# Keeping far-off work out of the opening stretch of a recorded schedule, and a longer guess for DMA transposes

## The chip, the cores and the metric

The kernel runs on one core of one Trainium2 chip, in one launch. The metric is the device time of that launch in microseconds (us), the median of several runs. Before the change it is 729.1 us (three runs, 729.02 to 730.64). Engines are named as in the profile: PE is TensorE (PEld its weight loads), DVE is VectorE, ACT is ScalarE, POOL is GpSimd, SP issues the DMAs.

## The reference

A pre-LayerNorm transformer block on 2048 tokens of width 1024: linear attention with 32 heads of 32, then a gated feed-forward part (F = 3584) with ReLU on the gate. Cut to what is computed:

```python
h  = x + A(_layernorm(x))          # A: qkv = x @ wqkv; phi(q), phi(k) = where(t > 0, t+1, exp(t)) + 1e-6
                                   #    kv = phi(k)^T v, z = sum phi(k); o = phi(q) kv / (phi(q) z + 1e-6); o @ wo
h2 = h + B(_layernorm(h))          # B: relu(x @ W_gate) * (x @ W_up) @ W_down
```

The inputs are bf16, and so is the output.

## The kernel before

The products are done as Strassen-Winograd blocks: seven products of half-size blocks in place of eight, for which DVE makes sums and differences of the blocks of the left operand (the normalized x, "left sums") and of the right operand (the weights). Each group of products ends in PSUM banks that ACT and DVE empty; until a bank has been emptied, PE can't start the next group in it.

All engine calls are recorded first, and then a planner inside the kernel gives them an order. It runs while the program is built, not on the chip: it has a guessed duration for each call, keeps a clock for each engine and one for the DMA wire, and always takes the call that can start first; among those that could start on an engine it takes the one with the smallest `late`, the latest start that by its guess holds nobody up. The order that comes out is fixed, and the engines follow it.

```python
class Plan:
    SEM = 100.0
    WINDOW = 6000.0
    AHEAD = 120000.0
    ...
    def schedule(self):
        nodes = self.nodes
        succs = self.order()            # sets v.late for each recorded call
        ...
        for i, v in enumerate(nodes):
            v.left, v.ready = len(v.preds), max(0.0, v.late - self.AHEAD) if v.dma else 0.0
            if not v.left:
                avail[v.eng].append(i)
        ...
            s, e, a = best
            now = [i for i in a if nodes[i].ready <= s]
            i = min(now, key=lambda i: (nodes[i].nom if e == "tensor" else nodes[i].late, i))
            ...
            v.start = s
            clock[e] = s + v.hold
            end = s + v.hold + v.lat
            if v.dma:
                wire = max(wire, s + v.hold) + v.dma
                end = wire + v.lat - v.dma + min(4000.0, max(0.0, 0.25 * (v.late - s)))
            ...                         # successors become ready at end
```

In the plan times are ns. A DMA transpose from SBUF to SBUF counts as a call of SP with `hold` 1250 and `lat` 2350 and no wire time (`v.dma` is 0).

These are the calls that matter for the opening. Tokens are handled in pairs of 128-token tiles (p and p + 8). Pair 0 is done with plain products, without the seven-product scheme, while the weights are still arriving:

```python
def left_sums(lo, n):                   # for tokens lo .. lo+n of both halves
    c = slice(lo, lo + n)
    a11, a12, a21, a22 = (XH[i][k][:, :, c] for i in range(2) for k in range(2))
    s1, s2, s4, s3 = (a[:, :, c] for a in (*XS, XS3))     # s3 lies over a21
    ...
    return [tt(s1, a21, a22, ALU.add), tt(s2, s1, a11, ALU.subtract),
            tt(s4, a12, s2, ALU.subtract), tt(s3, a11, a21, ALU.subtract)]     # four DVE calls

def k_phi(i, j, ps):                    # phi of a plain product of pair 0
    e = at(156 + 2 * i + j, [512])
    nc.scalar.activation(out=e, in_=ps, func=ACT.Exp)
    def post():
        phi_clamp(e)                                               # DVE, bf16 in place
        phi_join(pk0[:, i, j * 512:(j + 1) * 512], ps, e)          # DVE, reads the bank
    tick.do(lambda: post)

class Norm:                             # LayerNorm of one tile
    def finish(self, on_dve=False):
        self.rstd_()
        xn = self.xn
        (nc.vector if on_dve else nc.gpsimd).tensor_scalar(out=xn, in0=self.x, scalar1=self.negm[:], scalar2=self.rstd[:],
                                op0=ALU.add, op1=ALU.mult)
        nc.sync.dma_start_transpose(out=XI[self.i][:, :, self.r:self.r + P], in_=xn)
        ...

class Quad:                             # one group of seven products
    def p2(self):
        self.prod(self.D, 2, False)
        self.out["c22"](self.E, self.u3)     # DVE add of a bank and a copy; frees the bank
        self.out["c11"](self.D)
    ...

for p in range(1, NP):                  # NP = 8
    ...
    ls = left_sums((p + 1) % NP * P, P)      # at p = 7 these are the sums of pair 0
    ...
```

The left sums of pair 0 are recorded last in this loop (p = 7), since pair 0 needs them only for the products with the weights of q, which come after all of k and v.

Of the kernel before, what the change touches and what calls it, by code (L numbers as in the profile page):

```python
# [32 lines left out]
class Plan:  # L33
# [5 lines left out]
    SEM = 100.0  # L39
    WINDOW = 6000.0  # L40
    AHEAD = 120000.0

    class Node:
        __slots__ = ("eng", "calls", "preds", "hold", "lat", "open", "dma", "late", "ready", "left", "start", "nom")
# [155 lines left out]
    def schedule(self):  # L200
        nodes = self.nodes
        succs = self.order()
        engines = ("tensor", "vector", "scalar", "gpsimd", "sync")
        avail = {e: [] for e in engines}
        clock = {e: 0.0 for e in engines}
        for i, v in enumerate(nodes):
            v.left, v.ready = len(v.preds), max(0.0, v.late - self.AHEAD) if v.dma else 0.0
            if not v.left:
                avail[v.eng].append(i)
        pe = [i for i, v in enumerate(nodes) if v.eng == "tensor"]  # L210
        done, first, wire, out = set(), 0, 0.0, []
        while True:
            best = None
            for e in engines:
                a = avail[e]
                if not a:
                    continue
                if e == "sync":
                    for i in a:
                        v = nodes[i]  # L220
                        if v.late - max(clock[e], v.ready) > 6000.0:
                            v.ready = max(v.ready, wire - 2000.0)
                if e == "tensor":
                    while first < len(pe) and pe[first] in done:
                        first += 1
                    limit = nodes[pe[first]].nom + self.WINDOW
                    a = [i for i in a if nodes[i].nom <= limit]
                    if not a:
                        continue
                s = max(clock[e], min(nodes[i].ready for i in a))  # L230
                if best is None or s < best[0]:
                    best = (s, e, a)
            if best is None:
                break
# [3 lines that stand above are left out]
            v = nodes[i]  # L238
            if e != "tensor":

                soon = [j for j in a if s < nodes[j].ready < s + 0.5 * v.hold and nodes[j].late < v.late - 1500.0]
                if soon:
                    i = min(soon, key=lambda j: (nodes[j].late, j))
                    v = nodes[i]
                    s = v.ready
# [3 lines that stand above are left out]
            if v.dma:  # L249
                wire = max(wire, s + v.hold) + v.dma  # L250
                end = wire + v.lat - v.dma + min(4000.0, max(0.0, 0.25 * (v.late - s)))
            avail[e].remove(i)
            done.add(i)
            out.append(i)
            for j in succs[i]:
                w = nodes[j]
                r = clock[e] if w.eng == e else end
                w.ready = max(w.ready, r)
                w.left -= 1
                if not w.left:  # L260
                    avail[w.eng].append(j)
        assert len(out) == len(nodes)
        self.span = max(clock.values())
        return out
# [1303 lines left out]
```

## Time and profile before

The profiled execution spans 726.4 us. Its page and the windows of its trace say:

| stretch | PE busy | DVE busy | POOL busy | DMA share |
|---|---|---|---|---|
| whole span, 726.4 us | 714.9 us | 564.0 us | 78.2 us | q1: 54.4% of 16 engines |
| 0 to 10 us | 8.14 us | 4.77 us | 1.70 us | 0.78 |
| 10 to 20 us | 9.89 us | 9.68 us | 1.48 us | 1.14 |
| 20 to 28 us | 8.00 us | 6.83 us | 2.99 us | 0.38 |
| 28 to 32 us | 1.16 us | 4.00 us | 2.77 us | 0.44 |
| 32 to 60 us | 27.94 us | 21.85 us | 11.15 us | 0.66 |

A row is read across: in a stretch of 4 us (28 to 32) PE worked 1.16 us, and DVE all of it. A DMA share near or over 1 is read as full queues (the packets' times are added up). Nearly every call goes through one line of the recorder (L121), so lines of code don't tell groups apart, and the operation, the shape and the time of an instruction must.

### The profile page before, as it was taken

How to read it: one execution, taken by the hardware profiler on the slowest of the kernel's cores; microseconds unless marked ns; L12 is line 12 of the kernel's file. 1: busy time of each engine (PE TensorE's matmuls, PEld its weight loads, DVE VectorE, ACT ScalarE, POOL GpSimd, SP SyncE). 2: the span in 40 equal slices, each digit the busy share in tenths (PEclk: the TensorE clock that was granted, in tenths of full speed). 3: DMA queues.
4: the chain of work that ended last, by engine and by line, in shares of the span. 5: the costliest groups of instructions: out<-in, count | busy, mean ns of one | idle time of the engine just before them, and what ended most of it. 6: DMA issues, size and time to landing. Idle time of an engine off the chain costs nothing.

```text
span 726.4 us, 11220 instructions
## 1 busy us (share of the span) xinstructions
PE 714.9 (98%) x4163; PEld 396.9 (55%) x4163; DVE 564.0 (78%) x954; ACT 277.3 (38%) x540; POOL 78.2 (11%) x88
## 2 busy tenths in 40 slices
PE   8899999999999999999999999999999999999998
PEld 3344545444444444444444444444444688888887
DVE  6887745896897785566767968769858879899996
ACT  5788544666555443333333333333333220001100
POOL 1433000002202120000000000000000004101452
PEclk9999999999999999999999999999999999999999
DMA  9555505239776730446146585685681878777974
GB/s 286 157 120 115 148 1 180 54 84 222 160 158 151 142 85 1 122 140 188 51 143 190 154 254 159 197 261 178 206 262 50 268 262 221 205 271 233 247 79 60
DMA packets 156503, 117.40 MB, mean 162 GB/s; under 512 B 54944, under 2 KB 140192, under 8 KB 156320
## 3 DMA queue, kind: packets, MB, share of 16 engines
q1 hardware_dynamic: 148832, 113.01, 54.4%
q0 software_dynamic: 7616, 3.67, 4.9%
q8 instruction: 32, 0.52, 0.3%
q14 instruction: 23, 0.19, 0.1%
HBM read 70.52 MB, written 34.08 MB: 144 GB/s over the span
## 4 chain that ended last, share of the span: by engine, by line
PE 89%; DVE 5%; ACT 3%; DMA 2%; issue 1%; POOL 0%; DVEq 0%; ACTq 0%
PE psum L121 89%; DVE mem L121 4%; ACT mem L121 2%; DMA mem<-mem 2%; DVE tiny L121 1%; ACT tiny L121 0%; POOL mem L121 0%; DVE mem L549 0%; POOL tiny L121 0%; DVEq L121 0%; ACTq L121 0%
## 5 line engine op out<-in xcount | busy, mean ns | idle before, releaser
L121 PE MATMUL psum<-mem 128*128 128x512 f16 (+4 forms) x4147 | 714.0, 335 | 7.9 <-DVE mem L121 3.4
L121 PEld LDWEIGHTS <-mem 128*128 128x128 f16 (+1 forms) x4163 | 396.9, 98 | 325.6 <-issue 10.4
L121 DVE TENSOR_TENSOR mem<-psum,mem 128x512 f32<-128x512 f32 (+2 forms) x240 | 187.1, 792 | 100.8 <-ACT mem L121 67.0
L121 DVE TENSOR_TENSOR mem<-mem 128x512 f16<-128x512 bf16 (+8 forms) x400 | 241.6, 642 | 14.5 <-DMA mem<-mem 9.2
L121 ACT COPY mem<-psum 128x512 f32<-128x512 f32 (+2 forms) x124 | 92.7, 749 | 210.1 <-PE psum L121 202.4
L121 ACT COPY psum<-psum 128x512 f32<-128x512 f32 (+1 forms) x68 | 49.1, 722 | 160.6 <-PE psum L121 147.9
L121 POOL DMA_DIRECT2D out_dram<-mem x28 | 34.1, 1299 | 413.8 <-DVE mem L121 413.7
L121 ACT ACTIVATE mem<-psum 128x512 bf16<-128x512 f32 x90 | 53.6, 598 | 18.2 <-PE psum L121 17.7
L121 POOL TENSOR_SCALAR mem<-mem,tiny 128x1024 bf16<-128x1024 bf16 x28 | 38.2, 1364 | 197.0 <-ACT tiny L121 176.3
L121 DVE SCALAR_TENSOR_TENSOR mem<-mem 128x512 bf16<-128x512 bf16 (+1 forms) x71 | 57.6, 812 | 1.3
L121 DVE SCALAR_TENSOR_TENSOR mem<-psum,mem 128x512 bf16<-128x512 f32 x66 | 45.4, 687 | 11.9 <-PE psum L121 7.9
L121 ACT ACTIVATE mem<-mem,tiny 128x1024 bf16<-128x1024 bf16 x24 | 27.4, 1143 | 11.0 <-DVE tiny L121 5.8
L121 DVE TENSOR_SCALAR mem<-mem 128x512 bf16<-128x512 bf16 (+1 forms) x49 | 16.2, 331 | 18.2 <-ACT mem L121 18.0
L121 DVE TENSOR_TENSOR mem<-psum,tiny 128x384 bf16<-128x384 f32 (+1 forms) x48 | 22.9, 507 | 5.3 <-ACT tiny L121 3.9
L121 ACT ACTIVATE mem<-mem 128x1024 bf16<-128x1024 f32 (+1 forms) x23 | 24.3, 1056 | 6.3 <-DVE mem L121 6.2
L121 ACT ACTIVATE tiny<-tiny 128x1 f32<-128x1 f32 (+2 forms) x112 | 22.8, 206 | 9.2 <-DVE tiny L121 6.3
L121 ACT ACTIVATE tiny<-psum 128x12 f32<-128x12 f32 (+1 forms) x48 | 8.1, 169 | 13.9 <-PE psum L121 13.4
L121 DVE BATCH_NORM_STATS2 tiny<-mem 128x6 f32<-128x512 bf16 x16 | 10.2, 680 | 3.0 <-DMA mem<-in_A_x_dram 3.0
L121 ACT CAST mem<-psum 128x512 bf16<-128x512 f32 x18 | 10.4, 583 | 4.2 <-PE psum L121 3.7
L121 POOL TENSOR_SCALAR tiny<-tiny 128x1 f32<-128x1 f32 x14 | 4.4, 314 | 26.7 <-ACT mem L121 13.5
L121 ACT ACTIVATION_READ_ACCUMULATOR mem<-mem,tiny 128x1 f32 x24 | 4.5, 188 | 0.0
L121 DVE TENSOR_SCALAR tiny<-tiny 128x1 f32<-128x1 f32 x16 | 3.3, 209 | 0.3
(18 smaller groups left out, 14.4 us busy)
## 6 DMA issues: line engine op xcount, KB each, us to landing
l_dram<-mem SPq DMA_DIRECT2D x98, 128.0 KB, 2.3
mem<-l_dram SPq DMA_DIRECT2D x12, 896.0 KB, 6.1
mem<-in_A_x_dram SPq DMA_DIRECT2D x32, 256.0 KB, 3.0
mem<-in_B_W_up_dram SPq DMA_DIRECT2D x14, 512.0 KB, 5.4
mem<-in_B_W_gate_dram SPq DMA_DIRECT2D x14, 512.0 KB, 4.3
mem<-in_B_W_down_dram SPq DMA_DIRECT2D x28, 256.0 KB, 3.8
r_dram<-mem SPq DMA_DIRECT2D x56, 128.0 KB, 1.8
mem<-r_dram SPq DMA_DIRECT2D x8, 896.0 KB, 5.1
```

What stands on the lines that cost most here:

```text
L121: call = lambda: getattr(getattr(self.nc, eng), op)(*args, **k)
```

## The change

The change has two edits, both to the planner; no call is added, removed or altered.

1. A call that isn't PE's and whose `late` lies past 90 us isn't offered before 45 us of planned time. It is meant to keep work that is due much later, such as the left sums of pair 0, from being slipped into gaps of the opening, where the guesses are least sure.
2. A call of SP without wire time, which is a DMA transpose, is expected to end no sooner than 0.8 us after the planned wire is free, but at most 2.5 us later than guessed so far. It is meant to let the plan know that a transpose behind a full wire takes longer.

```diff
@@ class Plan
     AHEAD = 120000.0
+    OPENING = 45000.0
@@ def schedule
             v.left, v.ready = len(v.preds), max(0.0, v.late - self.AHEAD) if v.dma else 0.0
+            if v.eng != "tensor" and v.late > 2.0 * self.OPENING:
+
+                v.ready = max(v.ready, self.OPENING)
             if not v.left:
@@ def schedule
                 end = wire + v.lat - v.dma + min(4000.0, max(0.0, 0.25 * (v.late - s)))
+            elif e == "sync":
+
+                end = max(end, min(wire + 800.0, end + 2500.0))
             avail[e].remove(i)
```

What the two edits do to the order can be read from the two built programs. The orders on PE, ACT, POOL and SP are the same, instruction by instruction. On DVE six of 924 instructions stand elsewhere (times are those of the trace before, to find them by):

| instructions | shape | stood before | stand after | moved by |
|---|---|---|---|---|
| left sums s1, s2 of pair 0 | tensor_tensor, 128x512 | 13.49 and 14.01 us | behind the bank add of 51.03 us | edit 1 |
| left sums s3, s4 of pair 0 | tensor_tensor, 128x512 | 28.20 and 29.38 us | behind those two | edit 1 |
| clamp and join of k's block (0, 1) | tensor_scalar and scalar_tensor_tensor, 128x512 | 23.52 and 23.85 us | ahead of the sums of 21.25 us | edit 2 |

## The prediction

> **What bounds the kernel now.** I read the page first: the busy times, then the chain that ended last.
>
> ```profile
> PE 714.9 (98%) x4163; PEld 396.9 (55%) x4163; DVE 564.0 (78%) x954; ACT 277.3 (38%) x540; POOL 78.2 (11%) x88
> PE 89%; DVE 5%; ACT 3%; DMA 2%; issue 1%; POOL 0%; DVEq 0%; ACTq 0%
> ```
>
> PE is the bound: 714.9 of 726.4 us busy, and the change leaves every matmul and PE's order as it is. So only PE's idle time can move, 11.5 us or 1.6% of the span. A change of 2% is out of reach downwards. The second view is who PE waits for, between 10 and 60 us (total, times, longest):
>
> ```profile
> PE psum L121 <- DVE mem L121: 2.8, 1, 2.8
> ```
>
> It is one wait, and PE's timeline between 28.0 and 32.5 us places it (start, duration, operation, count, idle time before it):
>
> ```profile
> 31.83 1.02 PE L121 MATMUL psum<-mem 128*128 128x512 bf16 x4 [2.84 <-DVE mem L121]
> ```
>
> PE stops at 28.99 and goes on at 31.83, when DVE has emptied a bank. The third view is DVE's timeline before that:
>
> ```profile
> 21.25 2.35 DVE L121 TENSOR_TENSOR mem<-mem 128x512 f16<-128x512 bf16 x4 [1.10 <-DMA mem<-mem]
> 23.52 0.30 DVE L121 TENSOR_SCALAR mem<-mem 128x512 bf16<-128x512 bf16 x1
> 23.85 0.69 DVE L121 SCALAR_TENSOR_TENSOR mem<-psum,mem 128x512 bf16<-128x512 f32 x1
> 24.46 5.33 DVE L121 TENSOR_TENSOR mem<-mem 128x2048 f16<-128x2048 bf16 x6
> 29.71 1.27 DVE L121 BATCH_NORM_STATS2 tiny<-mem 128x6 f32<-128x512 bf16 x2
> 30.91 0.27 DVE L121 TENSOR_SCALAR mem<-mem 128x512 bf16<-128x512 bf16 x1
> 31.10 0.68 DVE L121 TENSOR_TENSOR mem<-psum,mem 128x512 f32<-128x512 f32 x1
> ```
>
> The reader is to see that no row after the first has idle time before it: from 21.25 to 31.78 DVE is one unbroken queue. The add at 31.10 is the c22 add that frees PE's bank; it ends at 31.78, PE starts 0.05 later. Its inputs were ready long before (ACT's copy of 27.30 ended at 27.88, and the clamp at 30.91 reads an exp that ended at 27.24). So the 2.84 us are DVE's queue alone. Ahead of the queue, DVE idled 1.10 us for a transpose.
>
> [...] the clamp at 30.91 lay ready for 3.67 us. [...] Here are a left sum of pair 0 and the POOL normalize beside it, each from a narrow window of its engine's timeline:
>
> ```profile
> 28.20 1.25 DVE L121 TENSOR_TENSOR mem<-mem 128x512 f16<-128x512 bf16 x1
> 29.38 0.41 DVE L121 TENSOR_TENSOR mem<-mem 128x512 f16<-128x512 bf16 x1
> ```
>
> ```profile
> 25.79 3.38 POOL L121 TENSOR_SCALAR mem<-mem,tiny 128x1024 bf16<-128x1024 bf16 x1 [2.12 <-ACT tiny L121]
> 29.17 1.60 POOL L121 TENSOR_SCALAR mem<-mem,tiny 128x1024 bf16<-128x1024 bf16 x1
> ```
>
> The same normalize takes 1.19 us beside bank adds or statistics (at 33.12, 55.06 and 56.90), the same sum 0.42. The 3.38 read as 2.2 us of waiting, and the 1.25 as 0.83 us of waiting until POOL, which ended at 29.18, let go.[...]
>
> **The change part by part.** Six DVE instructions move.
>
> (a) Clamp and join of k's block (0, 1), 23.52 to 24.46, move ahead of the sums at 21.25. They take 0.94 us of the queue there. Their exp was done by 16.67. In front of 21.25 lies the idle 1.10 us, from 20.15, and 0.30 + 0.69 with a 0.03 us step fit into it. The sums still wait for the transpose that lands at 21.23. So the queue after 23.52 comes 0.94 us forward.
>
> (b) Left sums s3 and s4, 28.20 to 29.71 (the statistics' start), leave the queue: 1.51 us, of which 0.83 is the wait for POOL.
>
> (c) Left sums s1 and s2 at 13.49 leave: 0.86 us. What follows, a tile's normalize at 15.49, has its ACT input only at 15.15, so that stretch gains 0.30 us. SP issues that tile's transpose behind a load that ends at 15.94 (16.05 before), so it hardly moves, and the gain becomes a longer idle before 21.25. For PE: nothing.
>
> Sum for the wait: 0.94 + 1.51 = 2.45 us. The c22 add would end at 29.33, PE start at 29.38, and 0.39 of the 2.84 us stay.
>
> (d) The four sums come back behind 51.03. What stands there now, DVE's and ACT's rows:
>
> ```profile
> 51.03 0.68 DVE L121 TENSOR_TENSOR mem<-psum,mem 128x512 bf16<-128x512 f32 x1
> 52.24 1.22 DVE L121 TENSOR_TENSOR mem<-mem 128x512 f16<-128x512 bf16 x3 [0.53 <-DMA mem<-mem]
> 55.63 0.21 DVE L121 BATCH_NORM_AGGREGATE tiny<-tiny 128x2 f32<-128x12 f32 x1
> 56.45 0.29 DVE L121 TENSOR_SCALAR mem<-mem 128x512 bf16<-128x512 bf16 x1 [0.61 <-ACT mem L121]
> ```
>
> ```profile
> 56.31 0.43 ACT L121 ACTIVATE tiny<-tiny 128x1 f32<-128x1 f32 x2
> 56.68 0.58 ACT L121 COPY mem<-psum 128x512 f32<-128x512 f32 x1
> ```
>
> Four sums take about 1.4 us at the steps of 0.34 to 0.45 seen elsewhere (1.54 for four at 45.05); 0.53 of it falls into the idle time, so the aggregate of 55.63 comes about 0.9 us later, ends at 56.7, and the small ACT pair that needs it starts there instead of at 56.31. ACT's copy of 56.68 stands behind it, and the matmul at 57.35 follows that copy by 0.08. So PE loses 0.3 us.[...] I take 0.5.
>
> After that PE's waits follow PE's own work: from 213 us to 723 the windows show it without a gap, and the semaphore events show loads landing 12 us or more ahead of the matmuls that need them. So a shift at 60 us stays a shift at the end.
>
> **The rivals.**
>
> *POOL takes what DVE gave back.* With the queue 1 us earlier and shorter, POOL's first normalize no longer runs against sums but beside the statistics (27.26 to 28.5 then), ends near 28.4, and the second starts at about the moment of the clamp, 28.46. The clamp[...] would wait up to 1.1 us, and the c22 add stands behind it. If POOL instead wins one step earlier, a 2048-wide difference waits the same. For it:[...] POOL's second normalize is ready from 28.22.[...] I give it 55 in 100; the gain at the wait is then 1.35 and not 2.45.
>
> *Nothing at the wait, as another engine ends it.* Against it: the copy and the exp behind the add are 3 us early, and the product before it is done at 28.99. I give it 5 in 100: about 729.
>
> *The returned sums cost as much as was won.*[...] 0.9 against 1.35. Then 728.7. Were the delay to spread to later banks, it would be slower, by tenths.
>
> **Range and chances.** Unblocked: 729.1 - 2.45 + 0.5 = 727.15. Blocked: 729.1 - 1.35 + 0.5 = 728.25. Weighted 45 to 55: 727.75, which I put at 727.7. The range runs from the best case with a small cost at 57 us (726.7, set to 726.6 for the spread of single runs) to nothing gained (729.1, set to 729.2). Over 2% is 14.6 us: faster can't come from 11.5 us of idle time, slower would need a new stop in a stage that this order hardly touches. I leave 0.5% for each.
>
> **What would show it.** In the profile after: PE's idle before the matmul of 31.83 falls from 2.84 to 0.4 (or to 1.4 to 1.5, with a clamp or a difference of over 1 us and POOL ending beside it); clamp and join stand in 20 to 21; the first POOL normalize is shorter than 3.38; four sums stand between 48 and 53, and a gap of 0.3 to 0.9 us on PE follows a few us later; all else keeps its length. The prediction is wrong if the wait near 29 us is ended by something other than DVE, if the clamp and join don't fit ahead of the transpose's landing, or if the gap near 57 us exceeds 1 us.

## The result and the profile after

The kernel before: 729.1 us, median of 5 runs (728.91 to 730.64). The changed kernel: 726.45 us, median of 5 runs (726.09 to 727.09). The medians differ by 2.65 us, or 0.4%. The ratio of the runs is 0.9961, with a 95% interval of 0.9947 to 0.9975, which is 2.8 us less. The predicted 727.7 lies 1.25 us above it, and the range of 726.6 to 729.2 misses it by 0.15 us. Where a kernel is said to take so many us less below, that is worked out from its ratio and the time of before beside it.

The page after, busy times and shares of the chain that ended last:

```profile
PE 714.4 (99%) x4163; PEld 396.7 (55%) x4163; DVE 563.9 (78%) x954; ACT 277.3 (38%) x540; POOL 77.8 (11%) x88
PE 85%; DVE 2%; DMA 2%; ACT 1%; issue 0%; POOL 0%; ACTq 0%
```

PE's busy time has hardly moved (714.9 to 714.4). The chain's share on DVE falls from 5% to 2%. Next, who PE waits for between 10 and 60 us (total, times, longest), where before there was one wait of 2.8 us for DVE:

```profile
PE psum L122 <- ACT mem L122: 0.6, 1, 0.6
PE psum L122 <- DVE mem L122: 0.5, 1, 0.5
```

PE's timeline from 28 to 60 us places both (start, duration, operation, count, idle time before it):

```profile
28.76 25.68 PE L122 MATMUL psum<-mem 128*128 128x512 bf16 x140 [0.54 <-DVE mem L122]
55.01 5.34 PE L122 MATMUL psum<-mem 128*128 128x512 f16 x24 [0.57 <-ACT mem L122]
```

The 2.84 us ahead of the matmul that waits for the c22 add are 0.54 now, and a new gap of 0.57 us stands near 55 us. DVE's timeline between 18 and 29 us shows why the first is short:

```profile
19.12 0.29 DVE L122 TENSOR_SCALAR mem<-mem 128x512 bf16<-128x512 bf16 x1
19.44 0.69 DVE L122 SCALAR_TENSOR_TENSOR mem<-psum,mem 128x512 bf16<-128x512 f32 x1
20.50 6.22 DVE L122 TENSOR_TENSOR mem<-mem 128x512 f16<-128x512 bf16 x8 [0.37 <-DMA mem<-mem]
26.64 1.28 DVE L122 BATCH_NORM_STATS2 tiny<-mem 128x6 f32<-128x512 bf16 x2
27.83 0.28 DVE L122 TENSOR_SCALAR mem<-mem 128x512 bf16<-128x512 bf16 x1
28.02 0.69 DVE L122 TENSOR_TENSOR mem<-psum,mem 128x512 f32<-128x512 f32 x1
```

Clamp and join stand at 19.12, in time that was idle; 0.37 us of it is left ahead of the sums. The clamp at 27.83 took 0.28 us, so POOL did not block it, and the c22 add ends at 28.71.

One thing about the start-up goes into every comparison below. The first 15 matmuls of PE, which do no work for the result, take 5.93 us in the trace before and 5.10 after, and in the traces of the experiments anything from 4.91 to 6.29, since the time at which they go from one every 0.43 us to one every 0.22 differs from run to run (6.3 us in the trace before, 4.6 after). Nothing that the change moves stands ahead of them.

### The profile page after: what moved, and what is told of

Same layout as the page of the kernel before. It is cut to its first block, busy times and chain, and to the rows that moved or that the text cites. A ratio compares the mean times of both kernels' runs of the same rounds, so it can differ in the third digit from the quotient of the medians.

```text
span 724.3 us, 11221 instructions
## 1 busy us (share of the span) xinstructions
PE 714.4 (99%) x4163; PEld 396.7 (55%) x4163; DVE 563.9 (78%) x954; ACT 277.3 (38%) x540; POOL 77.8 (11%) x88
## 4 chain that ended last, share of the span: by engine, by line
PE 85%; DVE 2%; DMA 2%; ACT 1%; issue 0%; POOL 0%; ACTq 0%
PE psum L122 85%; DVE mem L122 2%; DMA mem<-mem 2%; ACT mem L122 1%; POOL mem L122 0%; ACT tiny L122 0%; DVE tiny L122 0%; ACTq L122 0%
```

## The experiments

Theories, as the expectations name them. **A**: the order does what the prediction says, the true gain is 1.3 to 1.8 us, and the rest of the 2.65 is chance in the start and the spread of runs. **B**: the order is worth the whole 2.6 us. **C**, formed after the second group: PE's clock is cut to half for a while behind the long wait in about half of the runs, and shortening the wait takes that away as well. Times of before beside each group: 729.45 us (56 runs) for the first, 729.69 (23) for the second, 729.97 (15) for the third.

**The same two kernels again.** No edit. The kernel before:

> The kernel before, unchanged, for a second trace. In the first pair of traces PE's first matmuls (15 on junk data, which end at 7.11 us before and 6.28 us after) differ by 0.7 us although nothing in the order has changed up to there; then the wait near 29 us is 2.35 us shorter, the one near 57 us 0.73 longer and the one near 194 us 0.30 longer, which sums to -1.3 us without the start, while the medians differ by 2.65. Theory A (chance at the start): this trace shows PE's junk matmuls ending anywhere between 6.2 and 7.6 us, and the wait before the matmul of 31.83 again at 2.8 us. Theory B (the first trace understates): the wait is longer than 2.84 here, 3.5 us or more, since POOL holds DVE up more often.

The changed kernel:

> The changed kernel, unchanged, for a second trace. Theory A: the wait near 29 us is 0.5 us again and that near 57 us 0.7, and only the end of the junk matmuls moves, between 6.2 and 7.6 us; against the kernel before on this chip the median is lower by 1.3 us. Theory B: by 2.6 us.

Measured: before 729.18 us, ratio 0.9997 (0.9989 to 1.0004); its second trace has 2.46 us for the wait of 2.84. Changed 727.67 us (11 runs), ratio 0.9976 (0.9965 to 0.9986), which is 1.8 us less. The trace of this run of the changed kernel, and one more taken later, which was expected to show a gap near 55 to 57 us of 0.57 or of 1.45,

> The changed kernel once more: [...] the clock is full in either case, and the wait near 29 us is 0.5.

have the wait of 0.54 and 0.55 us near 29, but 1.45 us near 56 instead of 0.57. This is PE's timeline of the third trace:

```profile
28.93 25.68 PE L122 MATMUL psum<-mem 128*128 128x512 bf16 x140 [0.55 <-DVE mem L122]
56.07 4.26 PE L122 MATMUL psum<-mem 128*128 128x512 f16 x19 [1.45 <-ACT mem L122]
```

DVE and POOL around 52 us, first in the first trace, then in the third:

```profile
52.16 0.42 DVE L122 TENSOR_TENSOR mem<-mem 128x512 f16<-128x512 bf16 x1
51.99 1.48 POOL L122 TENSOR_SCALAR mem<-mem,tiny 128x1024 bf16<-128x1024 bf16 x1 [2.55 <-issue]
```

```profile
52.34 1.29 DVE L122 TENSOR_TENSOR mem<-mem 128x512 f16<-128x512 bf16 x1
52.17 1.19 POOL L122 TENSOR_SCALAR mem<-mem,tiny 128x1024 bf16<-128x1024 bf16 x1 [2.54 <-issue]
```

In both, POOL's normalize starts 0.17 us ahead of DVE's sum, while DVE's bank add still runs. In the first the sum takes its usual 0.42 and the normalize is stretched from 1.19 to 1.48; in the third the normalize takes 1.19 and the sum is stretched to 1.29, which is 0.87 us of waiting. The order is the same, POOL's lead is the same to a hundredth of a microsecond, and there are two outcomes: POOL's normalize takes 0.29 us longer, or DVE's sum 0.87. The sum belongs to the next tile and stands ahead of the statistics and the aggregate on which ACT's small pair and then its copy wait, so PE gets the 0.87 us in full.

**Each edit alone.** The first kernel has only the first of these two, the second only the second:

```diff
+            if v.eng != "tensor" and v.late > 2.0 * self.OPENING:
+                v.ready = max(v.ready, self.OPENING)
```

```diff
+            elif e == "sync":
+                end = max(end, min(wire + 800.0, end + 2500.0))
```

> Edit 1 alone: the four sums of pair 0 go behind 51 us, clamp and join of k's block (0, 1) stay behind the sums of 21.25. If DVE's queue sets the wait and the 0.83 us that the sum s3 waited for POOL goes with it: the wait falls from 2.84 to 1.3 us. If another DVE instruction of the queue waits for POOL in its place: 2.2 us. The gap near 57 us is there in full, 0.7 us. Net against before: -0.8 us, or 0 in the second case.

> Edit 2 alone: only clamp and join of k's block (0, 1) move, ahead of the sums of 21.25. If they fit into the idle time there: the wait near 29 us falls by 0.94, from 2.84 to 1.9 us, and no gap comes near 57 us; net -0.9 us. The sum s3 still stands in the queue, so its wait for POOL (1.25 us in place of 0.42) should be seen again, as POOL's normalize still meets the queue. If they push the sums back instead, the wait stays at 2.8.

Measured: the first edit alone 729.77 us, ratio 1.0007 (0.9995 to 1.0019); the second alone 728.2 us, ratio 0.9988 (0.9979 to 0.9997). The second does what term (a) says and no more: the wait is 2.00 us, and no gap follows near 57.

```profile
31.05 31.16 PE L122 MATMUL psum<-mem 128*128 128x512 bf16 x169 [2.00 <-DVE mem L122]
```

The first shortens the queue and loses more behind it than it gains at the wait. DVE's and POOL's timelines in its trace:

```profile
27.79 1.28 DVE L122 BATCH_NORM_STATS2 tiny<-mem 128x6 f32<-128x512 bf16 x2
28.98 1.12 DVE L122 TENSOR_SCALAR mem<-mem 128x512 bf16<-128x512 bf16 x1
30.02 0.67 DVE L122 TENSOR_TENSOR mem<-psum,mem 128x512 f32<-128x512 f32 x1
```

```profile
25.44 4.51 POOL L122 TENSOR_SCALAR mem<-mem,tiny 128x1024 bf16<-128x1024 bf16 x2 [2.18 <-ACT tiny L122]
```

Here, with one edit alone, the first rival of the prediction has come true: POOL's second normalize ends at 29.95, and the clamp of 28.98 took 1.12 us instead of 0.28. The wait stays at 2.12 us and the gap near 57 to 59 costs 1.45. Its windows showed something else, which the prediction did not have (columns: stretch, its length, PE busy and matmuls, PEclk, DMA share, GB/s):

```profile
31.00:32.00 1.00, 1.00 (x6) 0.98 0.81 113
32.00:33.00 1.00, 1.00 (x4) 0.50 1.09 321
33.00:34.00 1.00, 1.00 (x4) 0.50 1.13 252
34.00:35.00 1.00, 1.00 (x4) 0.50 0.87 243
35.00:36.00 1.00, 1.00 (x5) 0.82 0.99 181
```

PE is busy in every slice, but for some 3.4 us behind the wait the granted clock is 0.50, and the matmuls in it start 0.43 us apart instead of 0.22. (The count in brackets is of all matmuls that touch a slice, so it can't be read as a rate.)

**The wait for POOL, by itself.** In the kernel before, the normalize of tiles 2 and 10 on POOL is cut to 32 of 1024 columns; the rest of these tiles is left unnormalized. All orders stay.

```diff
-            (...).tensor_scalar(out=xn, in0=self.x, ...)
+            w = 32 if self.t % NP == 2 else D
+            (...).tensor_scalar(out=xn[:, 0:w], in0=self.x[:, 0:w], ...)
```

> The kernel before with POOL's normalize of tiles 2 and 10 cut from 1024 to 32 columns (the rest of those tiles is left unnormalized), all orders as before. If 0.83 us of the sum at 28.20 is a wait for POOL, that sum takes 0.42 instead of 1.25, the 2.84-us wait falls to about 2.0, and the kernel is 0.8 us faster than before. If the 1.25 us has another cause, the sum stays at 1.25 and the wait at 2.8.

Measured: 727.83 us, ratio 0.9983 (0.9974 to 0.9992). The six sums and differences that took 5.33 us from 24.46 take 4.50, and the wait is 2.05:

```profile
24.19 4.50 DVE L123 TENSOR_TENSOR mem<-mem 128x2048 f16<-128x2048 bf16 x6
30.74 31.45 PE L123 MATMUL psum<-mem 128*128 128x512 bf16 x171 [2.05 <-DVE mem L123]
```

The 0.83 us of term (b) were a wait for POOL. (In the second trace of before the six take 5.33 us again, from 24.17.) The same cut in the changed kernel, for tiles 5 and 13 (`== 5`), whose normalizes stand beside the returned sums:

> The changed kernel with POOL's normalize of tiles 5 and 13 (those beside the returned sums, at 47.1 and 52.0) cut from 1024 to 32 columns (the rest of those tiles is left unnormalized). If the gap near 56 us is the sums' own 0.3 us and the rest waits for POOL (0.4 us at s1, 0.87 us at the sum of the next tile in one trace of two), the gap falls from 0.57 or 1.45 to 0.1 to 0.3, and the kernel is 0.4 to 1.2 us faster than the changed kernel, 2.5 to 3.2 us faster than before. Rival: the gap is DVE's queue or ACT's, and stays above 0.5.

Measured: 726.43 us, ratio 0.9959 (0.9944 to 0.9973), 3.0 us less than before. PE's timeline:

```profile
29.40 25.68 PE L124 MATMUL psum<-mem 128*128 128x512 bf16 x137 [0.50 <-DVE mem L124]
55.25 5.12 PE L124 MATMUL psum<-mem 128*128 128x512 f16 x23 [0.17 <-ACT mem L124]
```

Of the gap near 55 us, 0.17 us is the work of the four sums, and all else is the wait for POOL. At the returned sums it is 0.4 us, in all three traces of the changed kernel; first that kernel's sums, then those of this one:

```profile
48.56 3.08 DVE L122 TENSOR_TENSOR mem<-mem 128x512 f16<-128x512 bf16 x7
49.20 2.68 DVE L124 TENSOR_TENSOR mem<-mem 128x512 f16<-128x512 bf16 x7
```

When the sum of the next tile at 52 us is stretched as well, 0.87 more is added.

**The sums put elsewhere.** The changed kernel, but the plan offers the four sums from 64 us on (91 us in the second):

```diff
+            if i in self.far:            # the four left sums of pair 0
+                v.ready = max(v.ready, 64000.0)
```

> The changed kernel, but the four left sums of pair 0 come back in DVE's idle time of about 2.5 us near 64 to 67 us instead of behind 48.5. Theory A (the changed kernel is truly 1.3 to 1.8 us faster: about 2.3 us won at the wait near 29 us, 0.6 to 1.6 us lost again at a gap near 56 us that the returned sums cause): that gap goes, and the kernel is 2.0 to 2.8 us faster than before, 0.6 to 1.2 us faster than the changed kernel measured beside it. Theory B (the changed kernel is truly 2.6 us faster, and the gap near 56 us costs nothing in the end): the time is that of the changed kernel. Rival within A: POOL's normalize near 52 us is released at another moment and blocks another DVE instruction, so that a gap of 0.5 us or more stays near 57 us though no sum stands there.

> The same with the four sums in an idle stretch near 91 us. If the place near 64 us was harmless, the two agree within 0.4 us; if sums near 64 us block or are blocked there, this one is faster by 0.3 to 0.9 us. Against before: 2.0 to 2.8 us faster by theory A.

Measured: 725.73 us, ratio 0.9953 (0.994 to 0.9965), and 726.03 us, ratio 0.995 (0.9936 to 0.9964). The gap near 56 is gone in both traces, and the waits near 29 us are 0.48 and 0.38. Third, beside the sums at 64 us, the two statistics of 26.64 stand behind the clamp and the c22 add:

```diff
+        stats = [i for i in out if nodes[i].op == "bn_stats"][6:8]
+        ...                            # bank: the next add out of a PSUM bank behind them
+        out = [i for i in out if i not in stats]
+        at = out.index(bank) + 1
+        out[at:at] = stats
```

> As sums_at_64, and the two halves of the bank statistics (BN stats, 1.28 us at 26.64) stand behind the clamp and the c22 add instead of ahead of them. If DVE's queue alone is the remaining wait near 29 us (0.54 us in the changed kernel), it vanishes, since the add then ends 1.2 us earlier: 2.5 to 3.3 us faster than before. Rival: the add then ends while something else[...] still holds it, or the statistics come too late for ACT's small pair and a later matmul waits the 0.5 us instead: then equal to sums_at_64.

Measured: 724.91 us, ratio 0.9939 (0.9927 to 0.9951), the fastest version of this study. Both of PE's waits are gone; its row in the timeline from 24 to 62 us has no idle time before it:

```profile
23.65 38.36 PE L123 MATMUL psum<-mem 128*128 128x512 f16 x206
```

These three went too well for A, which gave the sums at 64 and 91 us 2.0 to 2.8 us and the third version 2.5 to 3.3. The ratios say 3.4, 3.6 and 4.5, while the waits explain 2.2 to 2.7. About 1 us or more was missing from the account.

**The clock.** Each run comes with its mean granted clock. The runs of before fall into two kinds: in the first group 31 of 56 have 0.997 or 0.998 and a median of 730.0 us, the other 25 have 1.000 and 728.2. The count by kernel:

| kernels | PE's wait near 30 us | runs at 0.998 or lower | medians at 0.998 or lower, and above |
|---|---|---|---|
| before, four groups of runs | 2.5 to 2.8 | 64 of 116 | 730.0 and 728.2 (first group) |
| first edit alone; second alone; before with POOL cut | 2.0 to 2.1 | 23 of 54 | 729.2 and 727.6 (second edit) |
| second edit with POOL cut | 1.2 | 0 of 7 | - and 726.6 |
| before, wait filled | 0.8 | 0 of 9 | - and 727.0 |
| changed kernel and the four versions of it | 0 to 0.55 | 0 of 37 | - and 724.9 to 727.7 |

Two kernels were made for this. In the first, nine matmuls that do no work for the result stand in PE's queue ahead of the one that waits. They write a bank that is not in use then:

```diff
+                if mm == 123:
+                    for _ in range(9):
+                        self.nc.tensor.matmul(self.spare, lhsT=last.args["lhsT"], rhs=last.args["rhs"], start=True, stop=True)
```

> The kernel before, with nine matmuls of the operands of the matmul ahead, into a bank that is not in use then, put into PE's queue just ahead of the matmul that waits for the c22 add. They do no work for the result; PE is busy for 9 x 0.216 = 1.9 us of its wait, and that wait in the profile falls from 2.5-2.8 to 0.5-0.9 us. No other instruction moves. Theory C (PE's clock is cut to half for some 3.4 us in about half of the runs after a wait of 2 us or more, which costs about 1.7 us in those runs; what the change removes is partly this): no run, or hardly one, has a mean granted clock of 0.998, and the median is that of the runs of before with a clock of 1.000, 728.2 to 728.5, about 1.2 us faster than before. Rival: the 0.998 comes from elsewhere (the start, the last stages): half of the runs still have it, and the time is that of before or a little above.

Measured: 726.98 us, ratio 0.9968 (0.9956 to 0.998). PE's timeline:

```profile
28.93 2.11 PE L275 MATMUL psum<-mem 128*128 128x512 f16 x9
31.86 8.43 PE L121 MATMUL psum<-mem 128*128 128x512 bf16 x49 [0.82 <-DVE mem L121]
```

The matmul behind the wait starts at 31.86, as in the kernel before (31.83); nothing was won there. Yet no run has the lower clock. That separates the clock from the order. The rival is out. The median lies 1.2 us below the 728.2 that theory C gave; what is known of that stands below.

The second kernel adds the two ways of shortening the wait, the second edit and the cut normalize of tiles 2 and 10:

> The second edit alone (clamp and join ahead of the transpose), and POOL's normalize of tiles 2 and 10 cut from 1024 to 32 columns (the rest of those tiles is left unnormalized). If the terms of the wait add, it is 2.84 - 0.94 - 0.83, about 1.1 to 1.3 us. Theory C: a wait of 1.2 us still cuts the clock in a smaller share of the runs than the 2.0-us waits of edit2_only and before_pool_short (10 of 22 and 7 of 18 runs at 0.998), or in none; time about 727.0, 2.0 to 2.7 us faster than before. Rival: no share changes with the wait, half of the runs at 0.998, time 1.7 us faster than before.

Measured: 726.63 us, ratio 0.9963 (0.9949 to 0.9977). The wait is 1.19 us, so the terms add (2.84 - 0.94 - 0.83 = 1.07), and no run has the lower clock.

```profile
29.94 10.38 PE L124 MATMUL psum<-mem 128*128 128x512 bf16 x58 [1.19 <-DVE mem L124]
```

To see it in the kernel before, it was profiled three more times:

> The kernel before once more, one profile. By theory C there are two kinds of runs: with a mean clock of 1.000 no slice has less than full clock after the start; with 0.998 the slices from about 32 to 35.5 us have 0.50, behind the wait of 2.4 to 2.8 us, and matmuls there start 0.43 us apart instead of 0.21.

> The kernel before, one more profile, to see a run with a mean clock of 0.998. Theory C expects the 0.50 slices from about 32 to 35.5 us, right behind the wait of 2.5 us, and full clock everywhere else after the start. Rival: the half clock lies in another stage, and has nothing to do with this wait.

> As before_4: a second chance to see such a run, with the same expectation of each theory for the place of the half clock.

The first two had full clock (726.1 and 726.3 us of span), the third 0.998 (727.4 us). Its windows from 31 us, with the columns as above, and then its PE timeline:

```profile
31.00:32.00 1.00, 0.57 (x3) 1.00 0.68 117
32.00:33.00 1.00, 1.00 (x5) 0.68 1.05 308
33.00:34.00 1.00, 1.00 (x4) 0.50 1.13 274
34.00:35.00 1.00, 1.00 (x4) 0.50 0.38 141
35.00:36.00 1.00, 1.00 (x4) 0.62 0.92 178
36.00:40.00 4.00, 4.00 (x32) 1.00 0.45 91
```

```profile
31.43 4.87 PE L121 MATMUL psum<-mem 128*128 128x512 bf16 x14 [2.82 <-DVE mem L121]
```

In these windows the half clock stands right behind the wait. As an estimate from them, it lasts 3.4 us and takes 0.002 off the mean over 727.4 us, which is what this trace's 0.998 shows. In the windows of the first edit alone over its whole span, all stretches read 1.00 but that of 28 to 40 us (0.86) and the last, from 700 us on (0.97; it is 0.97 in the trace before and 0.98 after). Eight matmuls come 0.43 us apart instead of 0.22, which costs 1.7 us. In 55% of the runs that is 0.9 us on average.

**What stays open of the filled kernel.** Its ratio is worth 2.3 us, of which 0.9 is the clock. Its trace has another 1.0 us at 194 us, where PE waits 0.21 us instead of 1.21 (1.46 in the first trace of the changed kernel), behind a transpose that lands 1.4 us earlier.

> The kernel with the filled wait once more, for the 1.0 us that its first trace gains at the wait near 194 us (0.21 instead of 1.21), where a transpose landed 1.4 us earlier. If that belongs to the kernel, the wait near 194 is again 0.2; if it was chance, it is 1.1 to 1.5 as in all other traces.

The second trace again has 0.21 (at 193.52), so it belongs to this kernel. Only matmuls that move no other instruction were added; why the transpose lands earlier was not found.

**The account.** Each line takes the mean of before's five waits at full or half clock (2.84, 2.46, 2.51, 2.67, 2.82: 2.66 us), the kernel's own wait and gap from its trace, and the clock's 0.9 us (1.7 us by the share of its runs that have it).

| kernel | wait | gap near 56 | clock | sum | measured by the ratio |
|---|---|---|---|---|---|
| changed kernel | -2.1 | +0.6 or +1.45 | -0.9 | -2.4 or -1.6 | -2.8 and -1.8 |
| first edit alone | -0.5 | +1.45 | -0.2 | +0.7 | +0.5 |
| second edit alone | -0.7 | 0 | -0.2 | -0.9 | -0.9 |
| before, POOL cut | -0.6 | 0 | -0.3 | -0.9 | -1.2 |
| second edit, POOL cut | -1.5 | 0 | -0.9 | -2.4 | -2.7 |
| changed, POOL cut | -2.2 | +0.2 | -0.9 | -2.9 | -3.0 |
| sums at 64 us | -2.2 | 0 | -0.9 | -3.1 | -3.4 |
| sums at 91 us | -2.3 | 0 | -0.9 | -3.2 | -3.6 |
| sums at 64, statistics behind | -2.7 | 0 | -0.9 | -3.6 | -4.5 |

All sums but the last lie well inside the intervals; in the last, 3.6 is just at the end of its interval (3.6 to 5.3). But the kernels are faster than their sums in all rows but one, mostly by 0.2 to 0.4 us and by 0.9 in the last. What that remainder is stays open.

## Why the prediction was wrong

**The step that failed** is "So only PE's idle time can move, 11.5 us". PE's busy time moves too. In 64 of 116 runs of before the mean clock was lower, and the trace of one of this kind shows PE at half clock for 3.4 us behind the wait of 2.82. That costs 1.7 us in such a run and 0.9 on average. With the wait at 0.54 us, none of the changed kernel's 16 runs has it. The profile of before was one at full clock: its run took 728.12 us and its page shows full clock in all slices, while the three times it was set beside ran from 729.02 to 730.64. The clocks of those three are not on record; where they are, 55% of the runs of before have the lower clock. So the prediction took its terms from a full-clock trace and subtracted them from a median of mixed runs. The missing 0.9 us alone would have moved 727.7 to 726.8, inside the range and 0.35 from the result.

The rest of the 1.25 us is the weighting of the first rival: it had added 0.55 (727.15 to 727.7), and that rival did not come true. Against it stand 0.15 at the wait and 0.07 at the gap, which were larger than predicted. With all of them, 727.15 - 0.9 + 0.15 + 0.07 gives 726.47. That this meets 726.45 so closely is luck, and so is the side of the range's edge: the repeat gained only 1.8 us, and 729.1 less 1.8 is 727.3, inside the range.

**(a), clamp and join: right.** They stand at 19.12 to 20.13, and 0.37 us is left before the sums. The second edit alone lowers the wait to 2.00, against 2.84 - 0.94 = 1.90. From the mean of before's five traces, 2.66, the fall is 0.7 and not 0.94; one trace had stood for five that spread over 0.4 us.

**(b), s3 and s4: right in the changed kernel.** The wait for POOL in them is 0.83 us, by the kernel with the cut normalize. Without the second edit that wait was not won: 0.84 us of waiting moved from the sums to the clamp.

**(c): right.** Up to the wait, no matmul but those of the start-up comes earlier against its neighbours than before.

**The wait that stays** is 0.54 against 0.39.

**(d), the returned sums: the term was too small.** It said 0.5, up to 0.9. Traces have 0.57, 1.45 and 1.45. The sums' own share was put at 0.3 (the prediction's rows, 56.31 to 56.7, give 0.4) and measured 0.17. In the prediction's 0.5 stood, beside that share, the author's estimate of a wait for POOL's normalize at the first returned sum, and there is one (0.40 us: that sum takes 0.82). The prediction missed that POOL's next normalize then meets the sum of the next tile at 52.2, and costs 0.87 more in two traces of three. "The gap near 57 us exceeds 1 us" was named as a sign of being wrong, and it came; its sign is against the result, so it hid part of the clock's gain.

**The first rival, POOL on the clamp,** had 55 in 100. In three traces of the changed kernel and three of its versions with the same order there, it did not happen: PE's wait is 0.38 to 0.55 us in all six. In the first of them POOL's second normalize starts at 27.70, 0.13 us ahead of the clamp, and takes 1.31 us instead of 1.19, while the clamp takes its usual 0.28. In the one trace of the first edit alone the clamp waits (1.12 us). So POOL's normalize can hold the clamp up. The weight was the author's estimate and too high for this order; six traces don't give an exact one.

**A and B:** by the account, the order by itself is worth 0.7 to 1.5 us, near A's 1.3 to 1.8 and far from B's 2.6. A was wrong that the rest is chance: most of the rest is the clock.

## What to carry to other kernels

Before subtracting from a median, see that the profile and the timed runs are of one kind: between the two kinds of runs of before, 0.998 and 1.000, the medians differ by 1.3 to 1.9 us in 729, beside a change worth 1.8 to 2.8. A single wait of 2 us on PE cost up to 1.7 us beyond itself here, and either shortening it to 1.2 us or giving PE other matmuls in it took the surcharge away (0 of 7 and 0 of 9 runs). Work moved on DVE should here be put where no normalize on POOL runs beside it or beside the next link of a chain that PE waits for: a 512-wide sum that usually takes 0.42 us took up to 1.30 beside one. At 64 and 91 us the four sums cost PE nothing, and at 48 us they cost 0.6 to 1.45 us for 1.4 us of work.

## What the runs showed of the hardware

**PE's clock fell to half behind a long wait in some runs, for 3.4 us.** Two traces have it. In that of the first edit alone the wait is 2.12 us and ends at 30.75; in the fifth of before it is 2.82 and ends at 31.43. As an estimate from the shares of the slices (0.98 and 0.82 at the ends of the first, 0.68 and 0.62 of the second), the half clock lasts from 31.96 to 35.36 and from 32.36 to 35.76 us: 3.4 us each, from 1.2 and 0.9 us after PE goes on. In the first trace before and in that of the changed kernel the record of the granted clock has one stretch at full clock, 720.21 us long in both, from 6.3 and from 4.6 us to beyond the last matmul.

**The length of the wait alone doesn't decide it.** Six traces with waits of 2.00 to 2.84 us have no drop: four of before (2.84, 2.46, 2.51, 2.67), the second edit alone (2.00) and before with the POOL cut (2.05). By runs, the lower clock comes in 64 of 116 with a wait of 2.5 to 2.8 us, in 23 of 54 with 2.0 to 2.1, and in none of 53 with 1.2 or less. No kernel here has a wait between 1.2 and 2.0 us there, and what decides between two runs of one kernel was not shown.

**The PEclk column has no low value for the first microseconds,** where matmuls come 0.43 us apart: it reads 1.00 from 0 to 5 us in the trace before. The spacing of matmuls has to be read instead.

**Which of the two waits, DVE's sum or POOL's normalize, is not settled by the recorded starts alone.** With POOL's normalize recorded as starting 0.17 us ahead of DVE's 512-wide sum each time, the sum took its usual 0.42 us once (POOL's normalize 1.48, normally 1.19) and was stretched to 1.29 to 1.30 three times, twice in the changed kernel and once in the first edit alone (POOL's normalize 1.19 each time). What decides it was not shown.
